# Half of layer 1 of blocks 4 to 7 by seven products, with scores, masks and values at new places

## The chip, the cores and the metric

The kernel runs on one core of a Trainium2 chip. The metric is the device time of one execution in microseconds; several executions are taken, and the median counts. Engines are named as in the profile: PE is TensorE (its weight loads are PEld), DVE is VectorE, ACT is ScalarE, POOL is GpSimd, SP is SyncE, which issues most DMAs.

## The reference, cut to what matters

```python
# q, k, v: (8, 8, 576, 64) float32;  w_in: (512, 2048);  w_out: (2048, 512)
scores = np.matmul(q, k.transpose(0, 1, 3, 2)) / np.sqrt(64)
rel = pos[:, None] - pos[None, :]
scores = np.where((rel >= 0) & (rel < 64), scores, -1e9)      # sliding window, causal
attn = softmax(scores)
x = np.matmul(attn, v).transpose(0, 2, 1, 3).reshape(4608, 512)
h = np.maximum(x @ w_in, 0.0)
out = (h * h) @ w_out
```

So there is a windowed attention, and behind it a feed-forward of two layers with a squared ReLU. The multiplications of the two layers are nearly all of TensorE's work.

## The kernel before, in words

**Blocks.** The 4608 tokens are worked on as nine blocks of 512: block g (0 to 7) holds the first 512 tokens of batch g, and block 8 the last 64 tokens of all eight batches. For each block the kernel does attention for four units of two heads, then layer 1 (512 x 512 by 512 x 2048), then layer 2 (512 x 2048 by 2048 x 512). Matmul inputs are float16, sums are float32 in PSUM.

**Attention of a unit** (g, hp): `Sc` (L280) makes the scores, 16 matmuls of 64 columns, in one of two PSUM tiles `at0`, `at1`, and ScalarE's exponential (L300). `M` (L303) masks with a minimum on VectorE (L307). `A` is `AV` (L310, the product with the values, L323, which reads `v_ev` and, for odd half tiles, `v_od`, a copy of the values shifted by 64 rows) and `N` (L327, reciprocal and scaling on VectorE, L337). `X` (L340) transposes the result to `xT`: units 0 and 1 of blocks 3 to 7 by a DMA transpose on SyncE's queue (L350), the others with four TensorE matmuls (L358) and a copy (L118 on ScalarE, L120 on VectorE).

**Layer 1.** A plain step `F1(g, f)` (L365) makes 128 of the 2048 features: four matmuls of 512 columns (L372) into one of the two PSUM tiles of `ps_f1`, a maximum with 0 on VectorE (L375), a square on ScalarE (L376). There are 16 such steps in a block. Block 8 alone uses `L1S` (L505): layer 1 as a 2 x 2 block product with seven multiplications in place of eight (products 5, 1, 6, 2, 7, 3, 4), on sums of weights (`W_sum`, L472) and of `xT` (`X_sum`, L481) made on VectorE. A product for one group m of tiles is four matmuls of 256 columns (`product1`, L489, matmul at L494); sums between products go through the PSUM, copied from bank to bank by ScalarE (L118), and product 5 is kept in SBUF (`p5`).

**Layer 2.** Blocks 0 and 1 use `F2` (L404, L408): 16 quarters of four 512-column matmuls. Blocks 2 to 8 use `L2S` (L569): seven products for each half s of the tokens, 14 in all, each of eight matmuls of 256 columns (`product`, L458, matmul at L460) into `chain` or `side`, on weight sums T (`T_sum`) and sums S of h (`S_sum`, L448), which VectorE makes (L436). ScalarE writes scaled outputs to `osb` (L576), VectorE adds others to them (L579).

**Order.** The order of all instructions is written out by hand under a manual schedule. After a start part for blocks 0 and 1 there is a loop over n = 1 to 8. Stage n does layer 2 of block n, layer 1 of block n + 1 and attention of block n + 2 together. The string `order` names one step of layer 1 (`1`) or layer 2 (`2`) for each slot, 30 slots in most stages. `put(i, work)` sets other work ahead of slot i: two bursts of scores, each of two units, at slots 8 and 19 in most stages, the masks 3 and 4 slots later, both units' values 6 later, transposes 8 and 9 later; and the sums. All engines work in order, so what is put somewhere waits for what is ahead of it on its engine.

**Loads.** `next_part` (L759) loads one part (128 rows of q, k or v; 256 KB), casts it on GpSimd (L120) and, four parts later, transposes q or k with a DMA transpose (L245, the whole of q or k at once for blocks 4 on). With the last part of v it shifts the values on GpSimd (`shift_v_parts`, L230, six casts at L233). A line `total = ...` (L905) paces it by slots.

Of the kernel before, what the change touches and what calls it, by code (L numbers as in the profile page):

```python
# [15 lines left out]
def kernel(  # L16
# [28 lines left out]
    stp = ctx.enter_context(tc.tile_pool(name="stp", bufs=10))  # L45
# [6 lines left out]
    opool = ctx.enter_context(tc.tile_pool(name="opool", bufs=3))  # L52
# [54 lines left out]
    S_sb = hsum[:].bitcast(FP16).rearrange("p a b -> p (a b)").rearrange("p (k c d) -> p k c d", k=4, c=8)  # L107
# [43 lines left out]
    def new_v(g, half=0):  # L151
        ev[g, half] = vpool.tile([P, 4, H, VW], FP16, name="v_ev", tag="ev", bufs=3)
        nc.gpsimd.memset(ev[g, half][:, :, :, D:VW], 1.0 / X_SCALE)
        if g < B:
            od[g] = vpool.tile([P, 3, H, VW], FP16, name="v_od", tag="od", bufs=2)
            nc.gpsimd.memset(od[g][:, :, :, D:VW], 1.0 / X_SCALE)
# [3 lines left out]
    def whole(g):  # L160
        return g in seq[4:]
# [68 lines left out]
    def shift_v_parts(g):  # L230
        for m in range(3):
# [5 lines left out]
    def transpose_part(g, what, c):  # L237
        to = {"q": qT, "k": kT, "k2": kT}[what]
# [11 lines left out]
    XDMA = [(g, 0) for g in (3, 4, 5, 6, 7)]  # L250
# [114 lines left out]
    def F1(g, f, pool=ps_f1, tag="f1", into=None):  # L365
# [9 lines left out]
        nc.vector.tensor_scalar(out=hr[:], in0=hps[:], scalar1=0.0, scalar2=None, op0=ALU.max)  # L375
# [56 lines left out]
    def s_of(k, s):  # L432
        return S_sb[:, k - 1, :, 128 * s:128 * s + 128]
# [14 lines left out]
    def S_sum(g, k, s):  # L448
        if k == 1:
            minus(s_of(1, s), a_of(g, 1, 0, s), a_of(g, 1, 1, s), ALU.add)  # L450
        elif k == 2:
            minus(s_of(2, s), s_of(1, s), a_of(g, 0, 0, s))
        elif k == 3:
            minus(s_of(3, s), a_of(g, 0, 0, s), a_of(g, 1, 0, s))
        else:
            minus(s_of(4, s), a_of(g, 0, 1, s), s_of(2, s))
# [15 lines left out]
    def W_sum(k, engine, cc):  # L472
        if k not in wsums:
            t = tpool.tile([P, HP, 512], FP16, name="wS", tag="T")
            wsums[k] = t[:].rearrange("p a b -> p (a b)").rearrange("p (c f) -> p c f", c=2)
        a, b, op = {1: (w_of(1, 0), w_of(1, 1), ALU.add), 2: (wsums.get(1), w_of(0, 0), ALU.subtract),
                    3: (w_of(0, 0), w_of(1, 0), ALU.subtract), 4: (w_of(0, 1), wsums.get(2), ALU.subtract)}[k]
        cols = slice(cc * 512, cc * 512 + 512)
        minus(wsums[k][:, :, cols], a[:, :, cols], b[:, :, cols], op, engine)

    def X_sum(g, k):  # L481
        if k not in xsums:
            t = apool.tile([P, 2, 512], FP16, name="xS", tag="pm", bufs=4)
            xsums[k] = t[:, 0, :].rearrange("p (c t) -> p c t", c=2)
# [4 lines left out]
    def product1(to, m, a, b, start):  # L489

        for u in range(2):
            f = (2 * m + u) * P
            for cc in range(2):
                nc.tensor.matmul(to[:, u * HX:(u + 1) * HX], a[:, cc, f:f + P], b[:, cc, :],  # L494
                                 start=start and u == 0 and cc == 0, stop=cc == 1, skip_group_check=True)

    kept5 = {}
# [7 lines left out]
    def L1S(g, p, two, banks):  # L505
# [10 lines left out]
        def piece32(name):  # L516
            return stp.tile([P, 512], FP32, name=name, tag="st")
# [4 lines left out]
        def done(m, i, j, bank):  # L522
            hr = piece32("ls")
# [3 lines left out]
        def done5(m, i, j, bank, relu_on_act):  # L527
            y = piece32("ls")
            nc.vector.scalar_tensor_tensor(out=y[:], in0=bank, scalar=1.0, in1=kept5[m][:],
# [4 lines left out]
            else:  # L534
# [3 lines left out]
        to, lhs, rhs, start = {5: (1, wsums.get(1), xsums.get(1), True), 1: (0, w_of(0, 0), x_of(g, 0, 0), True),  # L538
                               2: (0, w_of(0, 1), x_of(g, 1, 0), False), 6: (1, wsums.get(2), xsums.get(2), False),
                               7: (2, wsums.get(3), xsums.get(3), False), 3: (1, wsums.get(4), x_of(g, 1, 1), False),  # L540
                               4: (0, w_of(1, 1), xsums.get(4), False)}[p]
# [21 lines left out]
    RELU = (True, False)  # L563
# [5 lines left out]
    def L2S(g, p, s, banks):  # L569
# [23 lines left out]
        elif p == 6:  # L593
            product(c, s_of(2, s), t_of(2), False)
            scaled(up[:, hi], c)
            flush()
        elif p == 5:
            product(pb, s_of(1, s), t_of(1), True)
            scaled(dn[:, hi], pb)
        elif p == 7:  # L600
            product(c, s_of(3, s), t_of(3), False)
            plus(dn[:, hi], c)
        elif p == 3:
            product(pb, s_of(4, s), b_of(1, 1), False)
# [27 lines left out]
    with tc.manual_schedule():  # L632
# [124 lines left out]
        pending = []  # L757

        def next_part():  # L759

            if parts_left:
# [3 lines left out]
                if w[0] != "v":  # L765
                    pending.append((g, w, c))
                elif g < B and c == 3:
                    shift_v_parts(g)
# [15 lines left out]
        def A(g, hp, i=1):  # L784
            AV(g, hp, i)
            N(g, hp)
# [37 lines left out]
        done = 12  # L824
        chain = ps_f2.tile([P, 512], FP32, name="chain", tag="f2")
        side = ps_tr.tile([P, 512], FP32, name="side", tag="tr")
        for n in range(1, NBLK):
# [114 lines left out]
```

## Time and profile before

| what | value |
|---|---|
| time, median of 3 (lowest to highest) | 293.88 us (293.29 to 294.34) |
| the profiled execution: time, span | 293.14 us, 291.3 us |
| granted TensorE clock | 1.00 |
| VectorE, ScalarE, GpSimd busy, whole span | 77%, 59%, 44% |
| plain layer-1 matmuls (L372) | 492 seen, 121.7 us |
| matmuls of `L1S` (L494) | 112 in the order of instructions |
| largest idle time of ScalarE, by what ended it | 80.1 us, VectorE's maximum at L375 |
| largest idle time of VectorE | 30.1 us, TensorE's product at L372 |

How to read it: the execution takes 1.8 us more than its span, which goes from the first instruction to the last. Busy time is a union, and matmuls are pipelined, so the mean duration of a matmul in a group is longer than the distance from one to the next. A group's row in the profile reads: line, engine, operation, out<-in, shapes, count, then busy us and mean ns of one, then idle us of the engine ahead of them and what ended it. A row of the timeline reads: start us, length us, engine, line, operation, names, shapes, count, and in brackets the idle time of that engine just before, with its releaser.

### The profile page before, as it was taken

How to read it: one execution, taken by the hardware profiler on the slowest of the kernel's cores; microseconds unless marked ns; L12 is line 12 of the kernel's file. 1: busy time of each engine (PE TensorE's matmuls, PEld its weight loads, DVE VectorE, ACT ScalarE, POOL GpSimd, SP SyncE). 2: the span in 40 equal slices, each digit the busy share in tenths (PEclk: the TensorE clock that was granted, in tenths of full speed). 3: DMA queues.
4: the chain of work that ended last, by engine and by line, in shares of the span. 5: the costliest groups of instructions: out<-in, count | busy, mean ns of one | idle time of the engine just before them, and what ended most of it. 6: DMA issues, size and time to landing. Idle time of an engine off the chain costs nothing.

```text
span 291.3 us, 7341 instructions
## 1 busy us (share of the span) xinstructions
PE 281.9 (97%) x2905; PEld 181.9 (62%) x2905; DVE 224.1 (77%) x397; ACT 171.7 (59%) x295; POOL 129.3 (44%) x216
## 2 busy tenths in 40 slices
PE   7889999999999999999999999999999999999994
PEld 5434445545444466667666766666666666888883
DVE  4957629688867787878779878877898889878782
ACT  3747846688465656465655565556454655587821
POOL 5869749963383368358347445553231000000002
PEclk9999999999999999999999999999999999999999
DMA  7999999979999999999999999999996013201015
GB/s 233 299 384 390 404 279 280 256 156 201 155 299 227 212 208 240 200 216 229 210 197 230 204 251 153 153 261 204 245 200 184 0 39 94 89 3 72 2 72 144
DMA packets 146849, 57.35 MB, mean 197 GB/s; under 512 B 131936, under 2 KB 138336, under 8 KB 146816
## 3 DMA queue, kind: packets, MB, share of 16 engines
q1 hardware_dynamic: 145344, 55.26, 87.6%
q10 hardware_dynamic: 1328, 1.25, 1.3%
q0 software_dynamic: 144, 0.39, 0.6%
q8 instruction: 22, 0.36, 0.5%
q14 instruction: 11, 0.09, 0.1%
HBM read 38.80 MB, written 9.44 MB: 166 GB/s over the span
## 4 chain that ended last, share of the span: by engine, by line
PE 88%; DMA 5%; SPq 2%; DVE 1%; ACT 1%; issue 1%; POOL 0%; DVEq 0%; ACTq 0%
PE hps L372 36%; PE chain L460 15%; PE side L460 12%; PE ops L408 4%; PE at L494 4%; PE at L323 3%; PE at L293 3%; DMA w_st<-in_moe_w_in_dram 3%; PE side L408 2%; PE chain L408 2%; PE more L460 2%; DMA hsum<-in_v_dram 2%; PE at L460 1%; PE tr L262 1%; PE at L358 1%; SPq L178 1%
## 5 line engine op out<-in xcount | busy, mean ns | idle before, releaser
L376 ACT ACTIVATE h<-hr 128x512 f16<-128x512 f32 x128 | 79.9, 630 | 80.4 <-DVE hr L375 80.1
L372 PE MATMUL hps<-xT,w_in_sb 128*128 128x512 f16 x492 | 121.7, 379 | 0.3 <-POOL w_in_sb L120 0.3
L375 DVE TENSOR_SCALAR hr<-hps 128x512 f32<-128x512 f32 x127 | 85.9, 687 | 31.5 <-PE hps L372 30.1
L372 PEld LDWEIGHTS <-w_in_sb 128*128 128x128 f16 x496 | 46.3, 98 | 42.7 <-POOL w_in_sb L120 1.6
L460 PEld LDWEIGHTS <-hsum 128*128 128x128 f16 x448 | 43.1, 98 | 11.8 <-DVE hsum L436 0.2
L120 POOL CAST v_ev<-st_v 128x512 f16<-128x512 f32 x29 | 20.8, 719 | 44.3 <-DMA st_v<-in_v_dram 44.3
L460 PEld LDWEIGHTS <-h 128*128 128x128 f16 x336 | 32.8, 98 | 9.1
L300 ACT ACTIVATE pm<-at 128x1024 f16<-128x1024 f32 x35 | 34.2, 1015 | 2.9 <-PE at L293 2.9
L120 POOL CAST k<-st_k 128x512 f16<-128x512 f32 x33 | 23.2, 704 | 27.1 <-DMA st_k<-in_k_dram 22.3
L401 POOL DMA_DIRECT2D out_dram<-osb x3 | 1.8, 596 | 64.8 <-ACT osb L576 63.5
L337 DVE TENSOR_TENSOR xs<-at,rden 128x512 f16<-128x512 f32 x36 | 24.9, 692 | 1.2
L460 PE MATMUL chain<-wsum,hsum 128*128 128x256 f16 x192 | 24.9, 273 | 0.0
L307 DVE TENSOR_TENSOR pm<-pm,mask 128x1024 f16<-128x1024 f16 x32 | 23.0, 731 | 2.1 <-ACT pm L300 2.1
L436 DVE TENSOR_TENSOR hsum<-h 128x1024 f16<-128x1024 f16 x28 | 20.3, 726 | 4.9 <-ACT h L376 4.8
L120 POOL CAST q<-st_q 128x512 f16<-128x512 f32 x25 | 18.6, 753 | 11.6 <-DMA st_q<-in_q_dram 11.1
L233 POOL CAST v_od<-st_v 64x512 f16<-64x512 f32 x30 | 21.5, 717 | 1.7
L408 PEld LDWEIGHTS <-h 128*128 128x128 f16 x128 | 11.6, 98 | 12.5
L323 PEld LDWEIGHTS <-pm 128*64 128x64 f16 x576 | 11.1, 110 | 6.1 <-DVE pm L307 3.4
L408 PE MATMUL ops<-w_out_sb,h 128*128 128x512 f16 x64 | 14.8, 380 | 0.0
L323 PE MATMUL at<-v_ev,pm 128*64 128x65 f16 x384 | 13.9, 198 | 0.3 <-ACT pm L300 0.3
L576 ACT ACTIVATE osb<-chain 128x256 f32<-128x256 f32 x36 | 13.4, 371 | 0.3 <-PE chain L460 0.3
L460 PE MATMUL side<-wsum,hsum 128*128 128x256 f16 x104 | 13.5, 273 | 0.0
(126 smaller groups left out, 373.3 us busy)
## 6 DMA issues: line engine op xcount, KB each, us to landing
st_k<-in_k_dram SPq DMA_DIRECT2D x32, 256.0 KB, 5.6
out_dram<-osb SPq DMA_DIRECT2D x32, 256.0 KB, 3.0
st_v<-in_v_dram SPq DMA_DIRECT2D x28, 256.0 KB, 4.4
st_q<-in_q_dram SPq DMA_DIRECT2D x24, 256.0 KB, 4.7
w_st<-in_moe_w_in_dram SPq DMA_DIRECT2D x4, 512.0 KB, 7.3
wsum<-in_moe_w_in_dram SPq DMA_DIRECT2D x4, 512.0 KB, 10.3
hsum<-in_moe_w_out_dram SPq DMA_DIRECT2D x4, 512.0 KB, 7.9
wsum<-in_moe_w_out_dram SPq DMA_DIRECT2D x4, 512.0 KB, 9.2
```

The source lines that it names most:

```text
L120: engine.tensor_copy(out=out, in_=in_)
L233: nc.gpsimd.tensor_copy(out=od[g][to:to + 64, m, :, 0:D], in_=st["v", g, c][of:of + 64, :].rearrange("p (h d) -> p h d", h=H))
L300: nc.scalar.activation(out=p[:, hh, :] if apart else p[:], in_=sc[hh] if apart else both[:], func=AF.Exp, scale=1.0 / float(D) ** 0.5)
L307: nc.vector.tensor_tensor(out=p[:], in0=p[:], in1=m.unsqueeze(1).broadcast_to([P, 2, 512]), op=ALU.min)
L323: nc.tensor.matmul(a[jj * 64:(jj + 1) * 64, hh, jp * VW:jp * VW + D + 1], pm[g, hp][:, hh, j * 64:(j + 1) * 64], vsel, start=True, stop=True)
L337: nc.vector.tensor_tensor(out=x.rearrange("p j h d -> p h j d"), in0=a[:, :, :, 0:D], in1=rden[:].unsqueeze(3).broadcast_to([P, 2, 4, D]), ...
L372: nc.tensor.matmul(hps[:], w_in_sb[:, c, f * P:(f + 1) * P], xT[g][:, c, :], start=(c == 0), stop=(c == DMC - 1))
L375: nc.vector.tensor_scalar(out=hr[:], in0=hps[:], scalar1=0.0, scalar2=None, op0=ALU.max)
L376: nc.scalar.activation(out=h2[g][:, f, :], in_=hr[:], func=AF.Square)
L408: nc.tensor.matmul(f2[g, ts][:], h2[g][:, f, ts * P:(ts + 1) * P], w_out_sb[:, f, :], start=(f == 0), stop=(f == FFC - 1))
L436: (engine or nc.vector).tensor_tensor(out=out, in0=a, in1=b, op=op)
L460: nc.tensor.matmul(to, a[:, f, :], b[:, f, :], start=start and f == 0, stop=f == HF - 1, skip_group_check=True)
```

## The change

1. **Layer 1 of blocks 4 to 7** (in stages n = 3 to 6, the list `HYB`): the features f with f mod 8 below 4 are done as two pairs m = 0, 1 in seven products each, with `pair_step`; the other eight stay plain steps. A pair has only two banks, both of `ps_f1`: b for products 5, 6, 3, and a, which is also c, for the others. Products come as 5, 1, 2, 6, 7, 3, 4.
2. `W_sum` works on half as many columns at a time (a pair of tile groups): the first half is made in stage 2 and the second in stage 6; sum 3 is written over weights, others into free parts of `hsum` and `w_out_sb`. Product 5 is kept in a free part of `w_out_sb`. `X_sum` is made for blocks 4 to 8. Sum S3 is written over h.
3. Product 7's end on VectorE is issued at once, and product 4 goes to bank c; one copy by ScalarE falls away (`copy(nc.scalar, a, c)`).
4. Plain steps may take their maximum on ScalarE (`on_act`): 9 in stage 1, 7 in stage 2, 2 in stage 3, 1 in each of stages 4 to 6.
5. **Places.** In the new stages the order is `111127272772277272` twice (36 slots; `7` is a product of a pair); scores at slots 2 and 20, masks 4 later, values 8 later, transposes 11 and 12 later; in stage 3 masks 1 and 4 later and values 6 and 9 later, one unit each. Stage 1: scores at 11 and 19, stage 2: at 11 and 20. Sums have new slots.
6. In the start part the mask of unit 3 of block 1 comes behind the values of unit 1, and a quarter of layer 2 stands between two transposes.
7. **Loads.** Nine buffers for parts in place of ten, four of `hr` in place of three; a slower pace; block 4 is transposed part by part; the shift of v waits until the next block's first q part is loaded and cast.

```diff
-    stp = ctx.enter_context(tc.tile_pool(name="stp", bufs=10))
+    stp = ctx.enter_context(tc.tile_pool(name="stp", bufs=9))
-    opool = ctx.enter_context(tc.tile_pool(name="opool", bufs=3))
+    opool = ctx.enter_context(tc.tile_pool(name="opool", bufs=4))
...
-        return g in seq[4:]
+        return g in seq[5:]
...
+        if on_act:
+            nc.scalar.activation(out=hr[:], in_=hps[:], func=AF.Relu)
+        else:
+            nc.vector.tensor_scalar(out=hr[:], in0=hps[:], scalar1=0.0, scalar2=None, op0=ALU.max)
...
+    def s_of(g, k, s):
+        return a_of(g, 1, 0, s) if k == 3 else S_sb[:, s, {1: 0, 2: 1, 4: 2}[k]]
...
             if p == 5:
-                kept5[m] = piece32("p5")
-                copy(nc.scalar, kept5[m][:], b)
+                copy(nc.scalar, five(m), b.rearrange("p (a b) -> p a b", a=4))
             elif p == 1:
                 copy(nc.scalar, b, a)
...
             elif p == 7:
-                copy(nc.scalar, a, c)
-                later["dve"].append(lambda m=m, c=c: done5(m, 1, 1, c, m < 2 or RELU[0]))
+                done5(m, 1, 1, c, (g, 2 * m) not in RELU)
             elif p == 3:
-                later["dve"].append(lambda m=m, b=b: done5(m, 0, 1, b, RELU[1]))
+                done5(m, 0, 1, b, (g, 2 * m + 1) not in RELU)
             else:
-                done(m, 1, 0, a)
+                done(m, 1, 0, c)
...
+    def pair_step(g, p, m):
+        if p == 5:
+            b, a = [ps_f1.tile([P, 512], FP32, name="hps", tag="f1") for _ in range(2)]
+            open_pair[m] = a[:], b[:], a[:]
+        L1S(g, p, (m,), {m: open_pair[m]})
...
                 elif g < B and c == 3:
-                    shift_v_parts(g)
+                    unshifted.append(g)
+                if unshifted and w == "q" and c == 0 or unshifted == [g3]:
+                    shift_v_parts(unshifted.pop())
...
-        A(g1, 0, 0); F(1, second); M(g1, 3)
-        A(g1, 1, 1); F(1, second); X(g1, 0)
-        A(g1, 2, 0); X(g1, 1, nc.scalar, *in_f1); A(g1, 3, 1); F(1, second)
+        A(g1, 0, 0); F(1, second)
+        A(g1, 1, 1); M(g1, 3); F(1, second); X(g1, 0)
+        A(g1, 2, 0); F(1, second); X(g1, 1, nc.scalar, *in_f1); A(g1, 3, 1)
...
+        HYB = (3, 4, 5, 6)
+        BURST = (2, 20)
+        MAT, AT, XAT = ((4, 4), (8, 8), (11, 12))
...
+            elif both:
+                steps = [lambda p=p, m=m: pair_step(one, p, m) for m in range(2) for p in (5, 1, 2, 6, 7, 3, 4)]
...
+                     "111127272772277272" * 2 if both else
...
+                        put(i + ((5, 5) if n == 1 else (6, 6) if n == 2 else (6, 9) if n == 3 else AT)[t], lambda u=u, t=t: A(*u, i=t))
...
-                total = 12 + (30 * (n - 1) + i + 1) * (len(load_list) - 12) // 140
+                total = 12 + (36 * (n - 1) + i + 1 - 0) * (len(load_list) - 12) // 176
```

More of the change, by code (lines that the diff above doesn't have):

```diff
@@ L237, in transpose_part @@
     def transpose_part(g, what, c):
+        if what == "v":
+            shift_v_parts(g)
+            return
         to = {"q": qT, "k": kT, "k2": kT}[what]
@@ L514, in wide, with piece32, five @@
             return t[:].rearrange("p (u t) -> p u t", u=2)
-        def piece32(name):
-            return stp.tile([P, 512], FP32, name=name, tag="st")
+        def piece32():
+            return opool.tile([P, 512], FP32, name="hr", tag="hr")
+        def five(m):
+            if m % 2 and g == B:
+                return wsums[1, 5].rearrange("p c h f -> p (c h) f").bitcast(FP32)
+            return w_out_sb[:, 0:4, HC:2 * HC].bitcast(FP32)
         def square(m, i, j, hr):
@@ L841 @@
                 second = [lambda p=p, s=s: L2S(g, p, s, (chain[:, 0:HC], side))
-                          for s in range(2) for p in ((1, 2, 6, 5, 7, 3, 4) if n == NBLK - 2 else ORDER)]
-            apart = n == NBLK - 2
+                          for s in range(2) for p in ORDER]
+            apart, both = n == NBLK - 2, n in HYB
+            steps = []
             if apart:
@@ L910 @@
                 catch_up(1, 1)
-            assert not at, at.keys()
+            for i in sorted(at):
+                for work in at[i]:
+                    work()
 _INS = ['q', 'k', 'v', 'moe_w_in', 'moe_w_out']
```

164 lines of the change are left out of this document (94 added, 70 removed).

## The prediction

> **What bounds the kernel now.** I read the page first, then the chain that ended last, then the stages one by one, and last the timeline around the steps that change.
>
> ```profile
> span 291.3 us, 7341 instructions
> PE 281.9 (97%) x2905; PEld 181.9 (62%) x2905; DVE 224.1 (77%) x397; ACT 171.7 (59%) x295; POOL 129.3 (44%) x216
> PE 88%; DMA 5%; SPq 2%; DVE 1%; ACT 1%; issue 1%; POOL 0%; DVEq 0%; ACTq 0%
> ```
>
> TensorE holds 88% of the chain. Its busy share alone proves little, since ends of matmuls are modelled, so I check a stage against its own work. The window (columns: stretch, length, then busy us and count of PE, PEld, DVE, ACT, POOL, clock, DMA, GB/s) is one stage, from one burst of scores to the same burst a block later; then the step lengths from the chain, then the timeline:
>
> ```profile
> 151.21:180.52 29.31, 29.31 (x314) 19.56 (x312) 23.53 (x43) 16.50 (x30) 16.60 (x24) 1.00 1.13 208
> ```
> ```profile
> 105.13 1.73 PE hps L372 x8
> 104.26 0.87 PE chain L460 x8
> 253.88 1.75 PE at L494 x16
> ```
> ```profile
> 122.00 1.03 PE L372 MATMUL hps<-xT,w_in_sb 128*128 128x512 f16 x4
> 122.96 0.64 PE L293 MATMUL at<-qT,kT 64*128 64x64 f16 x32
> 123.53 1.05 PE L460 MATMUL chain<-wsum,hsum 128*128 128x256 f16 x8
> 127.88 1.04 PE L460 MATMUL chain<-wsum,hsum 128*128 128x256 f16 x8
> 128.85 0.25 PE L323 MATMUL at<-v_ev,pm 128*64 128x65 f16 x4
> 129.35 0.20 PE L323 MATMUL at<-v_ev,pm 128*64 128x65 f16 x1
> 129.47 1.90 PE L372 MATMUL hps<-xT,w_in_sb 128*128 128x512 f16 x8
> ```
>
> The chain of waits gives step lengths: a 512-column matmul takes 1.73/8 = 0.216 us, so a plain layer-1 step (four) 0.864; a 256-column one 0.87/8 = 0.109, in layer 2 as in the products of layer 1. In the timeline a burst of scores takes 0.67 (from 122.00 + 0.864 to 123.53) and a burst of values 0.72 (from 127.88 + 0.87 to 129.47). About 0.09 of that is lost at each border: 128.75 to 128.85 going in, and 0.12 between the last value matmul and the next step, where the value matmuls follow each other by about 0.03. A stage is then 16 x 0.864 + 14 x 0.87 + 2 x 0.67 + 2 x 0.72 = 28.8 us, and two transposes of four short matmuls each are all that is left for the other 0.5 of the 29.31. So TensorE runs back to back in these stages at full clock (1.00), and only a shorter instruction stream, or a new wait, changes their length. VectorE has 5.8 us free in a stage, ScalarE 12.8.
>
> **The change, part by part.**
>
> *Fewer columns.* The order of instructions has 496 plain matmuls at L372 before and 368 after, and 112 at L494 before against 336 after. That is 128 x 0.216 = 27.65 us out and 224 x 0.109 = 24.45 us in: **-3.2 us**, 0.8 in each of the four stages.
>
> Whether that holds depends on the weights, because 96 more weight loads come with it (the group's last figures are busy us and mean ns of one):
>
> ```profile
> L460 PEld LDWEIGHTS <-hsum 128*128 128x128 f16 x448 | 43.1, 98 | 11.8 <-DVE hsum L436 0.2
> ```
>
> The 16 products at 253.88 had 16 loads and still took 1.75 us, so a load of 98 ns hides under a matmul of 109 ns. The Trainium skill, in "TensorE: Matmul & The Clock Gate", section "Part 3: Packing small matmuls", says that weight loads overlap running matmuls only when they go to another row group. This trace disagrees with that for full-height matmuls.
>
> *The pair's round trip.* Each of the eight new pairs of tiles (two in each of four stages) sends TensorE's product 1 to ScalarE, which copies bank to bank (L118), and product 2 then accumulates on the bank that was read. The only cover is one layer-2 product of 0.87 us. Rows for its price:
>
> ```profile
> L376 ACT ACTIVATE h<-hr 128x512 f16<-128x512 f32 x128 | 79.9, 630 | 80.4 <-DVE hr L375 80.1
> L300 ACT ACTIVATE pm<-at 128x1024 f16<-128x1024 f32 x35 | 34.2, 1015 | 2.9 <-PE at L293 2.9
> L576 ACT ACTIVATE osb<-chain 128x256 f32<-128x256 f32 x36 | 13.4, 371 | 0.3 <-PE chain L460 0.3
> L118 ACT ACTIVATE at<-at 128x512 f32<-128x512 f32 x4 | 2.3, 582 | 0.1
> L118 ACT ACTIVATE p<-at 128x512 f32<-128x512 f32 x4 | 2.2, 594 | 0.5 <-PE at L494 0.5
> ```
> ```profile
> 55.84 1.66 ACT L376 ACTIVATE h<-hr 128x512 f16<-128x512 f32 x3
> 250.22 1.04 PE L494 MATMUL at<-xS,wS 128*128 128x256 f16 x8
> 251.09 1.04 PE L494 MATMUL at<-xT,w_in_sb 128*128 128x256 f16 x8
> 251.34 1.08 ACT L118 ACTIVATE p<-at 128x512 f32<-128x512 f32 x2 [0.54 <-PE at L494]
> 264.95 1.20 ACT L118 ACTIVATE at<-at 128x512 f32<-128x512 f32 x2
> 265.18 1.04 PE L460 MATMUL side<-w_out_sb,h 128*128 128x256 f16 x8
> 266.20 1.03 PE L494 MATMUL at<-xS,wS 128*128 128x256 f16 x8
> ```
>
> A reader on ScalarE starts 0.25 us after the last matmul was issued (251.09 to 251.34), and TensorE starts 0.05 after a copy (266.15 to 266.20; there the wait cost 0.15 already, since the layer-2 product ended at 266.05). So the round trip is 0.25 + 0.58 + 0.05 = 0.88 against a cover of 0.87. That holds if ScalarE is free. Its queue ahead of the copy, counted from the second plain step of the half stage (out at 1.73, VectorE's maximum 0.69 long, so ready at 2.70): one square, two exponentials, two squares, one scaled output, the kept copy of product 5, the copy: 0.63 + 2.03 + 1.26 + 0.37 + 0.59 + 0.58 = 5.46, less six overlaps. Three squares took 1.66 instead of 1.89, which is 0.11 for each overlap; with 0.10 the copy ends at 2.70 + 4.86 = 7.56. TensorE asks for it at four plain steps 3.46 + scores 0.67 + three layer-2 products 2.61 + products 5 and 1 of 0.44 each = 7.61. Both paths arrive within 0.05 of the need. I take 0.04 per pair, **+0.3 us** for eight; the bounds are nothing (a wait cannot shorten the stream) and 0.6 each, if nothing overlaps (5.46 + 2.70 + 0.05 - 7.61). What waits behind it on TensorE is the whole stream. The other links have more room: product 7 needs the copy of product 6's sum, behind two layer-2 products (1.74 against 0.88), and product 4 needs VectorE to have read product 7's sum, behind product 3 and a layer-2 product (1.31 against 0.25 + 0.69 + 0.05).
>
> *Load of the other engines.* Per new stage ScalarE gets six copies (about 0.5 net), four maxima and one from the plain steps (0.53): 16.5 + 5.6 = 22.1 of 28.5 us. VectorE trades eight maxima for eight pair ends of the same length, gives one away, and gets four X sums:
>
> ```profile
> L375 DVE TENSOR_SCALAR hr<-hps 128x512 f32<-128x512 f32 x127 | 85.9, 687 | 31.5 <-PE hps L372 30.1 <-ACT h L376 0.8
> L529 DVE SCALAR_TENSOR_TENSOR ls<-c,p 128x512 f32<-128x512 f32 x4 | 2.6, 692 | 2.2 <-ACT at L118 2.2
> L436 DVE TENSOR_TENSOR xS<-xT,xS 128x512 f16<-128x512 f16 x2 | 0.8, 418 | 0.0
> ```
>
> That is 23.5 - 0.6 + 1.4 = 24.3 of 28.5 us. Both stay below their stage, so they cost nothing but lateness, which is the first rival. Stages 1 and 2 send 16 maxima to ScalarE, which has 12.8 us free per stage; W, S and T sums keep their number and move. All at nothing, covered by the same slack; if that cover failed, each late one would hold TensorE for up to its 0.69.
>
> *More borders.* The first of the four stages (layer 1 of block 4) has the values of its two bursts three slots apart (6 and 9) where they stood together. That is two splits, each with two borders of 0.09: **+0.4 us**.
>
> *Block 1's start.* The third mask (M) moves behind the second value unit, and a quarter of layer 2 stands between the transposes:
>
> ```profile
> 48.49 0.99 DVE L307 TENSOR_TENSOR pm<-pm,mask 128x1024 f16<-128x1024 f16 x1
> 49.63 0.69 DVE L337 TENSOR_TENSOR xs<-at,rden 128x512 f16<-128x512 f32 x1
> 50.38 0.40 PE L358 MATMUL xtr<-ident,xs 128*128 128x128 f16 x4 [0.56 <-DVE xs L337]
> ```
>
> The transpose waited for the normalization, which was behind the mask. With the mask behind it, it starts 0.9 earlier, and what is late next, the transpose of unit 2, has a quarter (0.86) ahead of it: **-0.55 us** (nothing to -0.7).
>
> *Loads and shifts.* SyncE loads at a slower pace (68 parts over 176 slots, not 140), with nine stage buffers for ten, block 4's q and k transposed in eight pieces, and scores at slot 2. GpSimd's shift of the odd value tiles (L233) now stands behind the cast of the next block's first q. For block 5 this is tight:
>
> ```profile
> 121.30 2.03 SPq L350 DMA_TRANSPOSE xT<-xs  x1
> 127.86 1.05 SPq L397 DMA_DIRECT2D out_dram<-osb  x2
> 98.00 2.07 SPq L206 DMA_DIRECT2D st_v<-in_v_dram  x3
> 100.17 4.58 SPq L245 DMA_TRANSPOSE kT<-k  x1
> 129.04 3.95 POOL L233 CAST v_od<-st_v 64x512 f16<-64x512 f32 x6
> ```
> ```profile
> st_q<-in_q_dram SPq DMA_DIRECT2D x24, 256.0 KB, 4.7
> kT<-k SPq DMA_TRANSPOSE x9, 5.8
> ```
>
> The order has on SyncE, after block 4's x transpose: one load, two stores, two loads, block 5's k transpose, the q load that the cast waits for. From the start of block 4's values at slot 17 (time 0): normalized at 2.3 (as from 128.85 on), x transpose to 4.3, stores to 5.4, loads to 7.5, k transpose issued to 12.1, the q load landed 4.7 later at 16.8, its cast done at 17.5 (0.7), the six shifts at 21.4. TensorE reaches block 5's values, slot 8 of the next stage, at 20.6 (eleven plain, eight layer-2 and two new steps, two bursts of scores, two of values and two transposes, by the lengths above). It reaches block 5's scores at 15.6, when k, issued at 7.5 and landed 5.8 later, is there. I take **+0.8 us** for the shift, with 0 and 2 as bounds; the value matmuls and all behind them on TensorE wait. For later blocks the same chain has over 5 us of room.
>
> *The rest* (product 4 onto another bank in the last layer-1 stage, sums of the last stage, in-place sums) removes four copies from ScalarE and lies beside TensorE's stream: nothing.
>
> **The sum.** The profiled execution took 293.14 us. -3.2 + 0.3 + 0.4 - 0.55 + 0.8 = -2.25, so 290.9 for such an execution. The median of the runs shown, 293.88, lies 0.74 above it; for the median I predict **291.6 us**.
>
> **Rivals.**
> - *ScalarE comes late to product 1's copy (the other side).* For: it works in order, and two exponentials of 1.0 stand ahead of the copy in each half. Against: three squares in 1.66 us show the overlap that I count on. With lateness d in each of eight pairs the time is 293.88 - 2.55 + 8d. It decides at d = 0.32; from 0.43 the kernel is slower by over 0.3%, and at the bound of 0.6 it takes 296.1. Chance 0.12.
> - *The same, half as late:* d between 0.2 and 0.43, the gain is used up: about 293.9. Chance 0.13.
> - *The shift for block 5 is late by its bound of 2 us.* For: a chain of five transfers and casts, of which each was taken at one row or a median. Against: nothing in it waits for TensorE after slot 17. 1.2 us more than forecast: 292.8. Chance 0.14.
> - *Weight loads that don't hide:* 96 more of 98 ns, +9.4, so 301.0. Against it stands the row at 253.88. The Trainium skill's sentence above is this rival. Chance 0.01.
> - *The forecast,* 290.1 to 292.6 for the median: 0.60.
>
> **How the numbers follow.** About 0.3% (0.9 us) is what a measurement of this kernel can tell from no change. Faster: forecast and late shift, 0.60 + 0.14, and 0.02 of the used-up case: 0.76; within 0.3%: the rest of that case and a little of the first rival, 0.12; slower: 0.12. The range goes from everything gained with nothing given back (293.88 - 3.2 - 0.55 = 290.1) to the used-up case, 294.0, and leaves out the slower ones.
>
> **What would show it.** The four stages should last 28.5 to 28.7 us, the stage at whose start block 4's layer 1 begins 0.4 more. Product 2 should start within 0.1 of the end of the layer-2 product before it; a gap there with ScalarE as its releaser means the first rival. A gap ahead of block 5's first value matmuls with GpSimd as the releaser means the third. The transpose at 50.4 should start without waiting for VectorE. I am wrong if stages keep 29.3 us with TensorE waiting, or if stages 1 and 2 grow.

## The result, and the profile after

| | before | after |
|---|---|---|
| median (lowest to highest), 10 runs each | 294.14 us (293.01 to 295.04) | 292.25 us (291.28 to 293.03) |
| ratio, 95% interval | | 0.9934 (0.9915 to 0.9953) |
| profiled execution: time, span | 293.14, 291.3 us | 291.48, 289.8 us |
| last matmul ends at | 287.37 us | 285.69 us |

The changed kernel is faster by 0.66%, about 1.9 us. The forecast was 291.6 us, from 290.1 to 294.0. The page of the changed kernel, first its span, busy engines and chain, then the weight loads of the products of layer 1 (busy us, mean ns of one, then idle us before them and its releaser):

```profile
span 289.8 us, 7571 instructions
PE 279.7 (97%) x3001; PEld 190.9 (66%) x3001; DVE 220.4 (76%) x391; ACT 203.5 (70%) x354; POOL 126.9 (44%) x216
PE 82%; DMA 6%; ACT 3%; DVE 3%; SPq 2%; issue 2%; POOL 0%; DVEq 0%; ACTq 0%
...
L521 PEld LDWEIGHTS <-w_in_sb 128*128 128x128 f16 x192 | 18.6, 98 | 2.9 <-issue 0.7
```

TensorE is still the bound at 97%, but its share of the chain went from 88% to 82%, while ScalarE and VectorE rose in it from 1% to 3% each. ScalarE is 32 us busier than before. The 96 more weight loads take 98 ns each and hide: the stages below are shorter, not longer. Three of the four changed stages, from burst of scores to burst of scores (columns as in the forecast's stage row):

```profile
134.93:164.10 29.17, 29.17 (x337) 21.97 (x337) 24.47 (x43) 22.44 (x42) 18.04 (x29) 1.00 1.16 220
164.10:192.71 28.61, 28.61 (x338) 21.91 (x338) 24.95 (x45) 22.62 (x42) 14.08 (x24) 1.00 1.04 215
192.71:221.94 29.23, 28.92 (x337) 21.89 (x336) 24.97 (x45) 22.50 (x42) 10.53 (x17) 1.00 1.14 220
```

The forecast said 28.5 to 28.7, and 0.4 more for the first. The second stage is there; the first is 0.1 over; the third is 0.5 over, and its PE busy time (28.92) shows that TensorE stood still in it. To see where, I took the distance from the start of each matmul to the start of the next. Where nothing disturbs them it is 0.21583 us for 512 columns and 0.10915 us for 256 in the mean; I call it the pitch. With 128 of the long ones fewer and 224 of the short ones more, the pitches add up to 3.18 us less than before, as the forecast's first term says. But the last matmul ends only 1.68 us earlier, so the excess over the pitches has grown by about 1.5 us. The experiments ask what this excess is.

### The profile page after: what moved, and what is told of

It reads as the page before. It is cut to its first block, busy times and chain, and to the rows that moved or that the text cites. A ratio compares the mean times of both kernels' runs of the same rounds, so it can differ in the third digit from the quotient of the medians.

```text
span 289.8 us, 7571 instructions
## 1 busy us (share of the span) xinstructions
PE 279.7 (97%) x3001; PEld 190.9 (66%) x3001; DVE 220.4 (76%) x391; ACT 203.5 (70%) x354; POOL 126.9 (44%) x216
## 4 chain that ended last, share of the span: by engine, by line
PE 82%; DMA 6%; ACT 3%; DVE 3%; SPq 2%; issue 2%; POOL 0%; DVEq 0%; ACTq 0%
PE hps L381 26%; PE chain L472 13%; PE side L472 10%; PE hps L521 8%; PE ops L420 5%; PE at L332 3%; PE at L302 3%; DMA w_st<-in_moe_w_in_dram 3%; PE side L420 2%; PE chain L420 2%; PE at L521 2%; PE more L472 2%; DMA hsum<-in_v_dram 2%; DMA st_v<-in_v_dram 1%; DVE hr L560 1%
## 5 line engine op out<-in xcount | busy, mean ns | idle before, releaser
L381 PE MATMUL hps<-xT,w_in_sb 128*128 128x512 f16 x364 | 87.3, 380 | 0.4 <-POOL w_in_sb L121 0.4
L388 ACT ACTIVATE h<-hr 128x512 f16<-128x512 f32 x96 | 59.3, 629 | 21.6 <-DVE hr L387 20.3
L387 DVE TENSOR_SCALAR hr<-hps 128x512 f32<-128x512 f32 x74 | 50.0, 687 | 21.9 <-PE hps L381 18.7
L381 PEld LDWEIGHTS <-w_in_sb 128*128 128x128 f16 x368 | 34.0, 98 | 36.3 <-POOL w_in_sb L121 1.7
L472 PEld LDWEIGHTS <-h 128*128 128x128 f16 x448 | 43.8, 98 | 9.0 <-issue 0.8
L309 ACT ACTIVATE pm<-at 128x1024 f16<-128x1024 f32 x35 | 34.1, 1012 | 3.4 <-PE at L302 3.4
L472 PEld LDWEIGHTS <-hsum 128*128 128x128 f16 x336 | 32.4, 98 | 4.6
L551 ACT ACTIVATE h<-hr 128x512 f16<-128x512 f32 x45 | 28.1, 627 | 10.0 <-DVE hr L555 9.4
L346 DVE TENSOR_TENSOR xs<-at,rden 128x512 f16<-128x512 f32 x36 | 24.9, 691 | 1.2
L472 PE MATMUL chain<-wsum,h 128*128 128x256 f16 x192 | 24.9, 273 | 0.1
L121 POOL CAST q<-st_q 128x512 f16<-128x512 f32 x25 | 16.3, 671 | 14.7 <-DMA st_q<-in_q_dram 14.3
L564 ACT ACTIVATE hr<-hr 128x512 f32<-128x512 f32 x21 | 13.1, 623 | 11.4 <-DVE hr L560 11.4
L521 PEld LDWEIGHTS <-w_in_sb 128*128 128x128 f16 x192 | 18.6, 98 | 2.9 <-issue 0.7
L420 PEld LDWEIGHTS <-h 128*128 128x128 f16 x128 | 11.7, 98 | 12.9
L616 DVE SCALAR_TENSOR_TENSOR osb<-side,osb 128x256 f32<-128x256 f32 x26 | 10.9, 420 | 6.6 <-ACT osb L613 4.7
```

Of the source, the lines that this page charges most:

```text
L121: engine.tensor_copy(out=out, in_=in_)
L309: nc.scalar.activation(out=p[:, hh, :] if apart else p[:], in_=sc[hh] if apart else both[:], func=AF.Exp, scale=1.0 / float(D) ** 0.5)
L346: nc.vector.tensor_tensor(out=x.rearrange("p j h d -> p h j d"), in0=a[:, :, :, 0:D], in1=rden[:].unsqueeze(3).broadcast_to([P, 2, 4, D]), ...
L381: nc.tensor.matmul(hps[:], w_in_sb[:, c, f * P:(f + 1) * P], xT[g][:, c, :], start=(c == 0), stop=(c == DMC - 1))
L388: nc.scalar.activation(out=h2[g][:, f, :], in_=hr[:], func=AF.Square)
L420: nc.tensor.matmul(f2[g, ts][:], h2[g][:, f, ts * P:(ts + 1) * P], w_out_sb[:, f, :], start=(f == 0), stop=(f == FFC - 1))
```

## The experiments

All are edits of the changed kernel, each compared with the kernel before on the same chip in five rounds. The medians of before were 293.52, 293.71 and 293.73 in the three groups. The changed kernel was not run again beside them, so kernels are compared with it by their ratios to before, not by their medians alone.

| kernel | median us | ratio to before, 95% |
|---|---|---|
| two layer-2 products behind product 1 | 292.7 | 0.9971 (0.9952 to 0.9990) |
| values together in the first stage | 292.12 | 0.9953 (0.9933 to 0.9973) |
| copy of product 1 twice | 296.46 | 1.0106 (1.0079 to 1.0133) |
| copy twice, two products behind | 296.67 | 1.0111 (1.0078 to 1.0145) |
| shift at once | 291.41 | 0.9918 (0.9890 to 0.9946) |
| block 1 in its old order | 292.63 | 0.9963 (0.9943 to 0.9982) |
| block 1, cast ahead of the mask | 291.83 | 0.9940 (0.9917 to 0.9962) |
| all plain | 296.45 | 1.0094 (1.0066 to 1.0121) |
| three edits | 291.19 | 0.9909 (0.9891 to 0.9926) |
| five edits | 291.05 | 0.9904 (0.9884 to 0.9923) |
| five edits, copy twice in six pairs | 291.4 | 0.9913 (0.9897 to 0.9930) |
| all plain, old order of slots | 294.23 | 1.0007 (0.9989 to 1.0026) |

### Is the gain the columns?

My theory was the forecast's: the gain is fewer columns, less what waits give back. The rival: it comes from the new places, loads and maxima on ScalarE.

```diff
-        HYB = (3, 4, 5, 6)
+        HYB = ()
-        WPUTS = {2: ((7, 1, 0), ...
+        WPUTS = {6: ((2, 1, 0), (8, 2, 0), (16, 3, 0), (18, 4, 0), (14, 1, 1), (22, 2, 1), (24, 3, 1), (28, 4, 1))}
...
```

The lines left out give stages 3 to 6 the places, sums and maxima of stage 2.

> Blocks 4 to 7 do all of layer 1 in plain steps, 30 slots with the places of stage 2 in stages 3 to 6; the weight sums for block 8 are all made in stage 6; all else as changed. Theory A (the gain is fewer columns and nothing else): the trace of the changed kernel has 3.17 us fewer columns, 0.4 in more borders and about 0.9 in waits of the pairs' products, so 1.9 us come back: 294.1 us, the kernel before within 0.3. Theory B (the gain comes from the rest, as the new places, the pace of loads or the maxima on ScalarE): 292.3 us. If the rest costs something, as a late shift, it is over 294.5.

It took 296.45 us, more than either theory said, as it would if the rest costs something. In the timeline of this kernel TensorE waits at the seam of two stages, four times alike (TensorE, then ScalarE; by the pitches the second product could have started at 164.40, 0.64 us before it did):

```profile
163.53 1.04 PE L472 MATMUL chain<-wsum,h 128*128 128x256 f16 x8
165.04 1.03 PE L472 MATMUL chain<-w_out_sb,h 128*128 128x256 f16 x8 [0.47 <-ACT osb L613]
```
```profile
164.61 0.38 ACT L613 ACTIVATE osb<-chain 128x256 f32<-128x256 f32 x1 [0.28 <-PE chain L472]
```

The last product of a block and the first of the next both use `chain`, with nothing between them, so TensorE waits for ScalarE to read it. I had taken the order of stage 2 without looking at its two ends. With the steps in turns as in the kernel before:

```diff
-                     "211211221211212121121122111222")
+                     ("211211221211212121121122111222" if n == 2 else "121212121212121121212121121122"))
```

> As the first plain kernel (blocks 4 to 7 all in plain steps), with layer 1 and layer 2 in turns in stages 3 to 6 as in the kernel before, not with three layer-2 products at the end of a stage and one at the start of the next, where TensorE waited 0.64 us four times for ScalarE to read the bank. Theory A (those waits, and not the rest of the change, made the first plain kernel slower than before): 296.45 - 2.6 = 293.9 us, the kernel before within 0.3. Theory B (the new places, loads and maxima cost the plain kernel 2 us by themselves): 296 us.

294.23 us, ratio 1.0007 (0.9989 to 1.0026): the kernel before. So the rest of the change, block 1's start included, is worth nothing by itself within 0.3% (0.8 us), and the seven products are the gain. The places that belong to the seven products were not tried apart from them. The Trainium skill ("TensorE: Matmul & The Clock Gate", section "Back-to-back issue gap") gives about 131 ns for a 512-column matmul in a sustained stream; as an estimate by that figure, 128 of them would be 16.8 us and the trade a loss. This trace disagrees, in the changed kernel too: eight of them take 1.74 us from their start to the next step's, 0.217 each.

```profile
135.50 1.90 PE L381 MATMUL hps<-xT,w_in_sb 128*128 128x512 f16 x8
137.24 1.04 PE L472 MATMUL chain<-w_out_sb,h 128*128 128x256 f16 x8
```

### What holds product 2: the round trip, or ScalarE's queue?

The forecast had both paths within 0.05 of the need. In the changed kernel, ScalarE's rows and TensorE's around one pair (the second of the second stage):

```profile
181.44 1.15 ACT L388 ACTIVATE h<-hr 128x512 f16<-128x512 f32 x2
182.48 0.38 ACT L613 ACTIVATE osb<-chain 128x256 f32<-128x256 f32 x1
182.75 0.61 ACT L119 ACTIVATE w_out_sb<-hps 128x512 f32<-128x512 f32 x1
183.40 0.58 ACT L119 ACTIVATE hps<-hps 128x512 f32<-128x512 f32 x1
```
```profile
182.70 0.60 PE L521 MATMUL hps<-xT,w_in_sb 128*128 128x256 f16 x4
183.14 1.04 PE L472 MATMUL chain<-wsum,hsum 128*128 128x256 f16 x8
184.03 0.60 PE L521 MATMUL hps<-xT,w_in_sb 128*128 128x256 f16 x4
```

The copy (L119, second row of it) ends at 183.98 and product 2 starts at 184.03; the layer-2 product ahead of it would have let it start at 184.01. In seven of the eight pairs product 2 starts 0.05 after the copy. Six of these are late by 0.02 to 0.07, one by 0.30, together 0.47 us. But why is the copy where it is? It stands 0.26 behind the end of product 1 (183.14) and 0.04 behind the kept copy, so both paths hold it. Doubling the copy shows that there is no cover left:

```diff
                 copy(nc.scalar, b, a)
+                if g < B:
+                    copy(nc.scalar, b, a)
```

> The copy of product 1 from bank to bank is made twice, one after the other, in each of the eight pairs of blocks 4 to 7 (0.60 us more of ScalarE each). Theory A (the cover of that copy is used up): product 2 and all of TensorE's stream behind it move by 0.6 in seven pairs and by 0.5 in the first, where 0.1 was free: 292.25 + 4.7 = 297.0 us, slower than the kernel before by about 1%. Theory B (ScalarE has 6 us free in a stage, so the copies hide): 292.25 us.

296.46 us; by the ratios, 1.0106 against 0.9934, about 5.0 us over the changed kernel: theory A, which said 4.7. TensorE at one pair of this kernel; seven pairs lose 0.63 to 0.84 us, the first nothing:

```profile
185.81 1.04 PE L472 MATMUL chain<-wsum,hsum 128*128 128x256 f16 x8
187.31 0.60 PE L521 MATMUL hps<-xT,w_in_sb 128*128 128x256 f16 x4 [0.47 <-ACT hps L119]
```

So the forecast's first rival, slower by lateness of ScalarE, was one copy of 0.6 us away. Next, twice the cover:

```diff
-                     "111127272772277272" * 2 if both else
+                     "111127722772277272" * 2 if both else
```

> One layer-2 product moves from ahead of product 1 to behind it, in each half of the four stages (order 1111 2 7 7 2 2 7 7 2 2 7 7 2 7 2). Theory A (the round trip through ScalarE's copy of product 1 is longer than its cover of one layer-2 product): in the changed kernel product 2 started 0.05 us after the end of that copy in seven of eight pairs, late by 0.02 to 0.07, once by 0.30, together 0.47 us. With 1.74 us of cover all of that goes: 292.25 - 0.5 = 291.8 us, and product 2 starts 0.109 after the last matmul ahead of it in all eight. Theory B (those gaps belong to something else, as a weight load or the bank that TensorE writes): the gaps stay, 292.25 us. Against both: product 1 comes 0.87 earlier onto the bank of the fourth plain step, whose maximum on VectorE ended about 0.1 ahead of that; if it is late, a new wait stands ahead of product 1, up to 0.7 in each pair.

> The copy made twice, and the order with two layer-2 products behind product 1. Theory A (what counts is the cover between product 1 and product 2, not ScalarE's load): counted from the end of product 5, the kept copy is at 0.25 to 0.84, the two copies end at 2.06, TensorE asks at 0.44 + 1.74 = 2.18, so the doubling costs nothing here: 291.8 us, as with the order alone. Theory B (the doubling costs because ScalarE is late in general, also with its squares and exponentials): about 0.6 for each pair again, 296.6 us.

My theory failed here. With the longer cover alone product 2 is on time, as theory A said, late by 0.005 us at most in all eight pairs; but in five of them it still starts just 0.05 after the copy, and the time did not fall (292.7 us). With the copy doubled as well the kernel still took 296.67, and six pairs lose 0.47 to 0.62 us. The timeline of the latter:

```profile
183.06 1.92 ACT L309 ACTIVATE pm<-at 128x1024 f16<-128x1024 f32 x2
184.86 1.15 ACT L388 ACTIVATE h<-hr 128x512 f16<-128x512 f32 x2
185.91 0.38 ACT L615 ACTIVATE osb<-chain 128x256 f32<-128x256 f32 x1
186.17 0.60 ACT L119 ACTIVATE w_out_sb<-hps 128x512 f32<-128x512 f32 x1
186.81 1.20 ACT L119 ACTIVATE hps<-hps 128x512 f32<-128x512 f32 x2
```
```profile
185.25 0.60 PE L521 MATMUL hps<-xT,w_in_sb 128*128 128x256 f16 x4
188.05 0.60 PE L521 MATMUL hps<-xT,w_in_sb 128*128 128x256 f16 x4 [0.46 <-ACT hps L119]
```

Product 1 is done at 185.69, but the copies start at 186.81: ScalarE works without a gap from the exponentials (L309) through two squares (L388) to the copies, none of which product 1 sets. My expectation had let the kept copy start when product 5 was done; it starts when the queue lets it. Its cover was doubled and its queue was not shortened. The longer cover also brought the wait that I had named as its danger, product 1 behind a maximum on VectorE. With the longer cover alone it makes product 1 late by 0.32, 1.06 and 0.28 us in the first three pairs, more than product 2 had lost; the longest, 0.90 us of it idle:

```profile
153.78 0.60 PE L521 MATMUL hps<-xS,hsum 128*128 128x256 f16 x4
155.28 0.60 PE L521 MATMUL hps<-xT,w_in_sb 128*128 128x256 f16 x4 [0.90 <-DVE hr L387]
```

If both paths bind, both have to go. A last pair of kernels moves the two squares behind the copy as well (and takes over the three edits told below):

```diff
+        if hold:
+            held.append(lambda: nc.scalar.activation(out=h2[g][:, f, :], in_=hr[:], func=AF.Square))
...
+                     ("111127272772277272" if n == 3 else "111127722772277272") * 2 if both else
...
                 copy(nc.scalar, b, a)
+                while held:
+                    held.pop(0)()
```

> As the kernel with three edits, and two more: in stages 4 to 6 two layer-2 products stand behind product 1, and in all four stages the squares of the third and fourth plain step are issued on ScalarE behind the copy of product 1. Theory A (the copy is late twice over, by the round trip and by ScalarE's queue, and only taking both away frees it): product 2 starts 0.109 after the matmul ahead of it in the six pairs of stages 4 to 6, with 0.5 us or more between the copy's end and its start; 0.4 us less than with three edits, 290.4 us. Theory B (the later squares hold a buffer or the next layer): new waits of VectorE for hr, the same time as with three edits or more.

> As the kernel with five edits, with the copy of product 1 made twice in the six pairs of blocks 5 to 7. Theory A (both paths into product 2 now have 0.5 us or more): the doubling, which cost 0.47 to 0.63 in each of these pairs with either path at its limit, costs 0.0 to 0.1 each: at most 0.6 us over the kernel with five edits. Theory B (ScalarE is late by its load, wherever the squares stand): 0.5 in each of six pairs, 3 us over it.

Five edits took 291.05 us, with the copy doubled 291.4; the intervals overlap. The doubling that cost each of these six pairs 0.47 to 0.74 us now costs nothing that TensorE's rows show. In the kernel with five edits and the doubled copy:

```profile
182.09 1.20 ACT L119 ACTIVATE hps<-hps 128x512 f32<-128x512 f32 x2
```
```profile
182.71 1.04 PE L476 MATMUL chain<-wsum,hsum 128*128 128x256 f16 x8
183.58 0.60 PE L525 MATMUL hps<-xT,w_in_sb 128*128 128x256 f16 x4
```

The copies end at 183.29 and product 2 starts on time, 0.87 after the product ahead of it. So round trip and queue were both at their limit: a longer cover alone could not hide the doubled copy, and with the queue shortened as well it did. A shorter queue alone was not run; that the round trip leaves no room rests on the pair above, where 0.89 us from the end of product 1 to the start of product 2 stand against a cover of 0.87. But five edits are no faster than three (291.19 us), and theory A's 0.4 us did not come: 0.39 us of waits went from the six pairs, but three of them lose 0.16 to 0.36 us ahead of product 1 instead, as with the longer cover alone.

### The shift of block 5's values

In the trace of the changed kernel, block 5's first values lose 0.15 us. From that I expected the forecast's +0.8 to be wrong.

```diff
-                    unshifted.append(g)
+                    shift_v_parts(g)
```

> The odd value tiles of every block are shifted on GpSimd at once, with the last part of v, as in the kernel before; all else as changed. Theory A (the trace of the changed kernel: block 5's values waited about 0.06 us in all for the shift): 292.2 us, and the 0.15 pause inside block 5's first values is gone. Theory B (the forecast's term: the late shift costs 0.8): 291.4 us.

291.41 us is the forecast's side, but by the ratios, 0.9918 against 0.9934, it is 0.5 us less than the changed kernel, and the intervals overlap. The traces tell the theories apart: my reading of the one trace was the mistake. The wait is there in all seven profiles with the late shift and the seven products, 0.15, 0.21, 0.86, 0.60, 0.86, 1.19 and 0.67 us (mean 0.65), and gone in this one. The longest is in the kernel with block 1 in its old order; there SyncE, GpSimd and TensorE read

```profile
127.02 5.36 SPq L254 DMA_TRANSPOSE kT<-k  x1
132.43 3.22 SPq L208 DMA_DIRECT2D st_q<-in_q_dram  x4
```
```profile
136.06 0.61 POOL L121 CAST q<-st_q 128x512 f16<-128x512 f32 x1 [3.10 <-DMA st_q<-in_q_dram]
136.74 4.99 POOL L239 CAST v_od<-st_v 64x512 f16<-64x512 f32 x6
```
```profile
141.78 0.19 PE L332 MATMUL at<-v_od,pm 128*64 128x65 f16 x1 [1.02 <-POOL v_od L239]
```

and in the changed kernel as profiled

```profile
126.27 4.71 SPq L254 DMA_TRANSPOSE kT<-k  x1
131.02 3.11 SPq L208 DMA_DIRECT2D st_q<-in_q_dram  x4
```
```profile
135.44 4.83 POOL L239 CAST v_od<-st_v 64x512 f16<-64x512 f32 x6
```

The chain is the forecast's: transpose, q load, cast, shift, values. The q load is issued 1.4 us later in the one than in the other: 0.75 because the transpose starts later, and 0.65 because its issue takes 5.36 us and not 4.71.

### Block 1's start

```diff
-        A(g1, 0, 0); F(1, second)
-        A(g1, 1, 1); M(g1, 3); F(1, second); X(g1, 0)
-        A(g1, 2, 0); F(1, second); X(g1, 1, nc.scalar, *in_f1); A(g1, 3, 1)
+        A(g1, 0, 0); F(1, second); M(g1, 3)
+        A(g1, 1, 1); F(1, second); X(g1, 0)
+        A(g1, 2, 0); X(g1, 1, nc.scalar, *in_f1); A(g1, 3, 1); F(1, second)
```

> The three lines of block 1's start in their order of before; all else as changed. Theory A (a new wait ahead of the second unit's values, 0.33 us idle, stands in place of the old one of 0.56 ahead of the transpose; whichever is there, about the same is lost): 292.4 us, and the stretch from the first unit's values to the third unit's is the same within 0.3. Theory B (the forecast's term, the new order is worth 0.55): 292.8 us.

292.63 us does not tell the theories apart; the timelines do. From the first unit's values to the first matmul of layer 1, the same work in each, before took 5.71 us and this kernel 5.70, with the old wait back in its place:

```profile
50.33 0.40 PE L367 MATMUL xtr<-ident,xs 128*128 128x128 f16 x4 [0.55 <-DVE xs L346]
```

The changed kernel took 5.49, because a new wait stands ahead of the second unit's values:

```profile
47.96 0.25 PE L332 MATMUL at<-v_ev,pm 128*64 128x65 f16 x4 [0.33 <-ACT v_ev L119]
...
50.78 0.39 PE L367 MATMUL xtr<-ident,xs 128*128 128x128 f16 x4
```

That wait is not in every execution: eight kernels with this order took 5.08 to 5.54 us for the stretch, 5.27 in the mean. Is it ScalarE, as the row says, or VectorE's cast, which the rows of three of the other kernels name?

```diff
-        M(g1, 2); cast_v_pair(g1, 1, nc.vector); Sc(g1, 3, i=1)
+        cast_v_pair(g1, 1, nc.vector); M(g1, 2); Sc(g1, 3, i=1)
```

> In block 1's start VectorE casts the second unit's values ahead of the third unit's mask (one call changes place). Theory A (the second unit's values at 47.96 waited for VectorE's cast, which ended at 47.90 behind a mask; VectorE was idle 0.31 ahead of that mask): the cast ends by 46.6, the wait of 0.33 goes with its refill, 0.4 to 0.5 in all: 291.8 us. Theory B (they waited for ScalarE's casts, as the row names them): the wait stays, 292.25 us.

The stretch is 5.08 with no wait here, and again 5.08 to 5.09 in the three other kernels with this edit: four of four without any loss, against three of eight. So it was the cast on VectorE. The time of 291.83 us alone could not show 0.2 us.

### Values together

```diff
-... (6, 9) if n == 3 else AT ...
+... (6, 6) if n == 3 else AT ...
```

> Both units' values stand together (slot 6 behind the scores) in the first of the four stages, where they stood 3 slots apart. Theory A (each border of a burst of values costs TensorE 0.09 going in and 0.10 coming out, whatever else happens): two splits less, 2 x 0.19 = 0.38 us, 291.9 us, and that stage goes from 29.17 to 28.8. Theory B (the split was needed: the second unit's mask or the shifted values are late, so the joined values wait): the border's 0.38 comes back as a wait ahead of the second unit's values; 292.25 us or more.

292.12 us, ratio 0.9953 against 0.9934: no gain over the changed kernel. The border's time comes back as a wait, as theory B said: at 145.36 TensorE is 0.47 us late, and the row names VectorE's sum of h (L448). Three edits together:

> Three edits together: the odd value tiles shifted at once, block 1's cast ahead of the mask, both units' values together in the first of the four stages; order of the pairs as changed. Theory A (in seven profiled executions the late shift held block 5's values by 0.15 to 1.19 us, 0.65 in the mean; the cast held block 1's by about 0.45; two splits cost 0.38): 292.25 - 0.65 - 0.45 - 0.38 = 290.8 us. Theory B (what a wait gives back is lost behind it, as the joined values ran into a wait of 0.47 for the sum of h that VectorE writes): 291.4 us or more.

291.19 us, ratio 0.9909 (0.9891 to 0.9926): faster than the changed kernel's 0.9934 by about what shift and cast gave in the traces, though the intervals overlap. Joining gave nothing. The first stage takes 28.96 us with the shift at once and joined values, and 29.00 with the shift at once and split ones. In the kernel with three edits:

```profile
142.20 1.04 PE L472 MATMUL side<-wsum,hsum 128*128 128x256 f16 x8
143.50 0.72 PE L472 MATMUL chain<-wsum,h 128*128 128x256 f16 x5 [0.26 <-ACT h L551]
```
```profile
141.56 0.69 DVE L346 TENSOR_TENSOR xs<-at,rden 128x512 f16<-128x512 f32 x1
142.16 0.68 DVE L555 TENSOR_SCALAR hr<-hps 128x512 f32<-128x512 f32 x1
142.76 0.68 DVE L448 TENSOR_TENSOR h<-h 128x1024 f16<-128x1024 f16 x1
```

With the second normalization (L346) now ahead of it, VectorE's sum S3 (L448) ends at 143.44, and the layer-2 product that reads it starts at 143.50. The row names ScalarE; VectorE ended last.

## Why the prediction was right, step by step

| term | forecast | measured | from |
|---|---|---|---|
| fewer columns | -3.2 | -3.18 | pitches of the matmuls |
| round trip of the pairs | +0.3 | +0.47 | starts of product 2 in eight pairs |
| more borders | +0.4 | +0.38 | four borders of 0.09 to 0.10 |
| block 1's start | -0.55 | -0.44 | 5.71 to a mean of 5.27 in eight executions |
| late shift | +0.8 | +0.65 | mean of seven executions |
| the rest | 0 | +0.36 | excess in the last layer-1 stage, 0.26 to 0.62 |
| sum | -2.25 | -1.76 | medians: -1.9 |

Sign and mechanism are right, and so is the point from which ScalarE's rival decides: the forecast put the two paths at 7.56 and 7.61 for the same moment, and the runs found both at their limit. Three terms were mis-sized by 0.1 to 0.2 each. The shift's +0.8 came near in part by luck: in the changed kernel the cast of q began 3.5 us after the transpose was issued, not 4.7, but the six shifts took 4.83 us, not 3.95. The forecast's round trip of 0.04 per pair held in six pairs; one, the second of the third stage, lost 0.30, in all six profiles with that order and one copy, because the copy started 0.33 after the kept copy although product 1 was done. Why, stays open:

```profile
211.70 0.60 ACT L119 ACTIVATE w_out_sb<-hps 128x512 f32<-128x512 f32 x1
212.63 0.58 ACT L119 ACTIVATE hps<-hps 128x512 f32<-128x512 f32 x1 [0.33 <-ACT w_out_sb L119]
```

The step that failed is "The rest ... lies beside TensorE's stream: nothing". In the last layer-1 stage (block 8) TensorE's excess over its pitches was 0.26 us before and 0.62 after, in every profile with seven products in blocks 4 to 7. Of this, 0.25 and 0.29 us stand at two places. TensorE, then VectorE, then ScalarE, in the changed kernel:

```profile
249.11 1.04 PE L521 MATMUL at<-xT,w_in_sb 128*128 128x256 f16 x8
249.98 1.29 PE L472 MATMUL chain<-w_out_sb,h 128*128 128x256 f16 x8
...
259.04 1.04 PE L472 MATMUL side<-w_out_sb,hsum 128*128 128x256 f16 x8
260.21 1.03 PE L472 MATMUL chain<-wsum,h 128*128 128x256 f16 x8
```
```profile
258.54 1.28 DVE L567 SCALAR_TENSOR_TENSOR h<-hr 128x512 f16<-128x512 f32 x2
259.74 0.41 DVE L616 SCALAR_TENSOR_TENSOR osb<-chain,osb 128x256 f32<-128x256 f32 x1
```
```profile
249.19 0.62 ACT L551 ACTIVATE h<-hr 128x512 f16<-128x512 f32 x1
249.71 0.59 ACT L119 ACTIVATE w_out_sb<-at 128x512 f32<-128x512 f32 x1
```

At 260.21 the product waits for VectorE to read `chain` (L616, which ends at 260.15). Ahead of that read stand four ends of products (0.68 each) that the change issues at once where they came later before, and the two in-place steps of L567. But the two plain kernels have this stage in its new form too. They show the same 0.29 at this place and nothing else, 0.3 in all, so against the 0.26 of before this place adds next to nothing.

What is added comes with the seven products, at the first place, where eight matmuls take 1.29 in place of 1.04. The same timeline, opened at 250.3, shows the second of them:

```profile
250.35 0.92 PE L472 MATMUL chain<-w_out_sb,h 128*128 128x256 f16 x7
```

The row has no releaser, but it starts 0.05 us after ScalarE's copy of product 5 into `w_out_sb` (L119) ends at 250.30, as product 2 does after its copy, and so it does in all eleven profiles with the seven products. The copy starts 0.60 after product 5 (249.11), because squares of block 7's last pair (L551) are still ahead of it; in the plain kernels it starts 0.25 after product 5, and TensorE doesn't wait. So what the forecast put beside TensorE's stream was again ScalarE's queue ahead of a copy. This is read from the traces: no run moved these squares or tried the stage in its old form.

The third stage's other wait, 0.34 us at 203.97 for VectorE's sum for product 4, appears in only one other profile, that of the doubled copy.

The forecast's 291.6 against 292.25 closes within 0.1: the rest +0.36, the pairs +0.17, block 1 +0.11, the shift -0.15, together 0.49; and the kernel before itself measured 294.14 here, 0.26 above the median that the forecast started from. The table's means come from several kernels; in the two profiled executions alone block 1 gives -0.22, the shift +0.15 and the wait at 203.97 +0.34, and with the other terms that is -1.70, against the 1.68 us by which the last matmul ends earlier. Of "what would show it", the transpose at 50.78 waits for nothing, as said, but the wait moved ahead of the second values; the second stage's 28.61 is as said, and so is product 2's start within 0.1 in all pairs but one; stages 1 and 2 grew by 0.2 us at most (from block 1's first layer-1 matmul to the start of stage 3, 81.41 us against 81.23); GpSimd as releaser appears in five of the seven profiles with a late shift, not in the first.

## What to carry to other kernels

When two paths arrive together, slack for one of them buys little: here the longer cover alone left a doubled copy as dear as before. List every path into the waiting instruction, and give slack to all of them or to none. Trading large matmuls for more small ones paid just the columns saved here, where the weight loads hide, so the question is what the freed stream then runs into; borders and small waits took back 1.9 of 3.2 us, and block 1's new order gave 0.4 of its own. A wait at the end of a chain of DMAs should be judged over several profiles: one trace showed 0.15 us where the mean was 0.65.

## What was not expected of the hardware

The same DMA transpose on SyncE's queue (k of block 5) took 3.70 to 5.82 us to issue in the thirteen kernels with the new loads, one execution of each, and the load behind it started 0.04 to 0.05 us after its end each time. VectorE's cast of 128x512 in block 1 took 0.89 us in the changed kernel, 0.73 before, and 0.42 to 0.76 us in the four kernels where it stood ahead of the mask; what makes the difference was not tried.
